# Last column of layer 1 reordered in the twelve seven-product phases, with decodings, W_in's second column, token pieces and stores at other times

## The chip, the cores and the metric

The kernel runs on one core of a Trainium2 chip. The metric is the time of one execution on the device in microseconds (us); it is given as the median of three runs. The engines are TensorE (PE, with its weight loads as PEld), VectorE (DVE), ScalarE (ACT), GpSimd (POOL) and SyncE (SP), which here only issues DMAs.

## The reference

Three stages follow each other, each reading the output of the one before; all of it is float32.

```python
# 1. decayed linear attention, q k v of shape (2, 8, 768, 64)
for t in range(S):
    state = gamma * state + einsum('bhd,bhe->bhde', k[:, :, t], v[:, :, t])
    y[:, :, t] = scale * einsum('bhd,bhde->bhe', q[:, :, t], state)
# 2. mixture of experts on x (1536 x 512), 8 experts, w1 512 x 1024, w2 1024 x 512
P = exp(x @ w_gate - max)              # then 8 rounds of row and column scaling
out = sum over e of P[:, e] * (maximum(x @ w1[e], 0) @ w2[e])
# 3. dense layer, w_in 512 x 2048, w_out 2048 x 512
h = x @ w_in
out = (maximum(h, 0) + alpha * minimum(h, 0)) @ w_out
```

## The kernel before

**Tiling.** The attention fills the first 46 us or so. Then 20 phases follow (`PHASES`, L35), one for each pair of a half of the tokens (768 of 1536) and an expert, or a half of w_in's and w_out's hidden columns. Phases 0 to 7 are half 0 with experts 0 to 7; their first layer is done by the seven products of Strassen and Winograd, their second in the ordinary way. Phases 8 to 15 are half 1 with the experts, and 16 to 19 the dense layer; in these twelve (`FAST`) both layers use seven products. Every float32 product is three matmuls on high and low parts (`mm3`, L300 to L303: high by high is L301, high by low L302, low by high L303).

**A phase.** A phase of the twelve is a row of 56 places on TensorE, each of six matmuls of 128 x 128 by 384 columns. Products of layer 1 are named (column j, product p), with four columns of seven products; column 3 is the last. Units 0 to 27 are layer 2. `fast_order` (L1195 to L1199) and `sequence` (L1201) write the row by hand. Layer 1's sums come out in PSUM; ScalarE copies them out (L947, L967) and VectorE adds to them (L962), or, in the dense layer, makes the slope of the activation (L918 on ScalarE, L919 on VectorE). The blocks b110, b111, b120, b121, b210 and so on are quarters of the hidden layer: `t1` (L1029), `t2` and `t3` (L1033) combine them. Layer 2 then needs fourteen operands hs0 to hs13, each a high half made by ScalarE (`hhigh`, L1055) and a low half made by VectorE (`hlow`, L1063, or L1033 and L1035 for some). Unit u reads hs number u // 2 (hs0 is first read at place 26 or 27, hs1 at 30, hs3 at 34, hs5 at 38, hs12 at 52) with the first and third of its matmuls on the high half and the second (L302) on the low half. So a wait of L302 for hs is one for a low half.

**What sets the order of the other engines.** `step(ph, pos, fn)` (L1209) hangs a piece of work behind the place pos of phase ph; a place of 60 or more belongs to the next phase. Each engine runs what it was given in that order, and a DMA of SP waits in the same way.

**The work hung there, as far as the change touches it.**

- `decode_at` (L1215): W_out and W_in come in a packed form. A piece is loaded (rd, L835), and five VectorE operations (L845, L847, L850, L863, L866) and one of ScalarE (L855) unpack it. Only phases from 1 on have them. Phase 8 has three decodings, at places 5, 17 and 29.
- `w1_at` (L1234): prepares one column n of a later phase's W1 or W_in. Its raw piece (raw0_n) is loaded by `w_load`; four sums (L139) build the combined blocks, then ScalarE makes the high half of the parts a, c and b (L162) and VectorE the low half (L172). The low half of b issues the load of column n + 2 into the buffer that it frees. In phase 15, n + 4 and n + 5 are columns 64 and 65, the first two of W_in for phase 16.
- `x_keep` (L352) and `x_fetch` (L377): pieces of the tokens' combinations. `x_keep` combines them on ScalarE (L366) and GpSimd (L362, L370) and stores them; they are called from phase 16 on, at keys 20, 26, 32 and so on counted in places. `x_fetch` loads them in the phase ahead of their use.
- GpSimd's other work in the twelve phases is the sums of W2's combined blocks (L280, four to a block); the operation L270 of VectorE writes the block dw before them.
- `w1_keep` (L180): stores a prepared piece of W1, so that phases 8 to 15 can load it again (c1). The first ones are collected in `unkept`.

## Time and profile before

| | |
|---|---|
| median of three runs | 1265.24 us |
| lowest and highest | 1264.0 and 1266.26 us |
| the profiled execution's own time | 1265.2 us |
| its span in the trace | 1263.5 us |
| TensorE busy | 1253.4 us, 99% |
| VectorE busy | 999.7 us, 79% |
| ScalarE busy | 652.6 us, 52% |
| GpSimd busy | 454.2 us, 36% |

The profile is one execution taken by the hardware profiler. Its span runs from the first to the last instruction of the trace; 1.7 us of the execution's time lie around it. A group of rows gives the start, the duration, the engine, the line of the code, the operation, and the tiles written and read; in brackets stands the idle time ahead of it on its engine and what ended it.

### The profile page before, as it was taken

To read this page: it belongs to the slowest core of one execution; us is meant where nothing else is said; L and a number is where in the kernel's file an instruction comes from. 1 tells how busy PE (TensorE), PEld (TensorE's weight loads), DVE (VectorE), ACT (ScalarE), POOL (GpSimd) and SP (SyncE) were. 2 spreads that over 40 slices of the span, in tenths; PEclk is the share of its full clock that TensorE was granted. 3 is DMA by queue.
4 is the path that set the end of the run, shared out by engine and by line. 5 is a ranking of instruction groups with operands and counts; after the bars stand their busy time and mean duration, and the time that the engine had idled before them with its cause. 6 is when DMAs were issued, how large, how long until landed. Compare 5 with 4: busy or idle time off the path is not lost.

```text
span 1263.5 us, 20609 instructions
## 1 busy us (share of the span) xinstructions
PE 1253.4 (99%) x7358; PEld 1189.7 (94%) x7358; DVE 999.7 (79%) x1538; ACT 652.6 (52%) x1211; POOL 454.2 (36%) x408
## 2 busy tenths in 40 slices
PE   9999999999999999999999999999999999999998
PEld 7888999989898989899999999999999999999998
DVE  6676888888888888859596967787786989796866
ACT  5644635444444444456455454546464647656573
POOL 5733252526161616101033433252423565551200
PEclk9999999999999999999999999999999999999999
DMA  9784999999999999899999989898989976695615
GB/s 356 260 288 132 329 327 358 326 350 333 341 335 344 336 337 337 278 331 382 329 328 320 337 291 331 290 357 293 355 290 342 332 252 199 231 375 190 215 53 183
DMA packets 230869, 378.15 MB, mean 299 GB/s; under 512 B 16960, under 2 KB 135792, under 8 KB 230768
## 3 DMA queue, kind: packets, MB, share of 16 engines
q1 hardware_dynamic: 230768, 376.85, 87.1%
q8 instruction: 58, 0.95, 0.3%
q14 instruction: 43, 0.35, 0.1%
HBM read 242.54 MB, written 132.67 MB: 297 GB/s over the span
## 4 chain that ended last, share of the span: by engine, by line
PE 93%; DVE 3%; DMA 2%; ACT 1%; issue 0%; SPq 0%; DVEq 0%; ACTq 0%
PE B L302 8%; PE B L301 8%; PE B L303 8%; PE o L301 7%; PE o L303 7%; PE o L302 7%; PE A L301 7%; PE A L302 7%; PE A L303 7%; PE D L302 4%; PE D L301 4%; PE D L303 4%; PE E L301 4%; PE E L303 4%; PE E L302 4%; PE y L581 1%
## 5 line engine op out<-in xcount | busy, mean ns | idle before, releaser
L1055 ACT ACTIVATE hs<-b 128x768 fp32r<-128x768 f32 x168 | 139.5, 842 | 66.5 <-DVE b L1033 18.2
L139 POOL TENSOR_TENSOR raw<-raw 128x256 f32<-128x256 f32 x128 | 125.3, 989 | 100.2 <-DMA raw<-wd 60.7
L1063 DVE TENSOR_TENSOR hs<-b,hs 128x768 fp32r<-128x768 f32 x120 | 119.9, 999 | 9.4 <-ACT hs L1055 9.1
L237 POOL TENSOR_TENSOR pr<-pr 128x256 f32<-128x256 f32 x52 | 52.1, 1002 | 188.7 <-ACT ex L855 62.2
L301 PE MATMUL A<-xh,W 128*128 128x384 f32 x320 | 107.8, 337 | 0.2 <-ACT B L947 0.2
L303 PE MATMUL A<-xh,W 128*128 128x384 f32 x320 | 107.2, 335 | 0.0
L302 PE MATMUL A<-xl,W 128*128 128x384 f32 x320 | 107.0, 335 | 0.0
L162 ACT ACTIVATE W<-raw 128x512 fp32r<-128x512 f32 (+1 forms) x138 | 94.0, 695 | 19.3 <-DVE raw L139 19.3
L302 PE MATMUL B<-hs,ws 128*128 128x384 f32 x288 | 96.8, 336 | 2.0 <-DVE hs L1063 2.0
L370 POOL TENSOR_TENSOR xs<-b,xs 128x384 fp32r<-128x384 f32 x21 | 29.5, 1404 | 191.6 <-ACT xs L366 144.5
L303 PE MATMUL B<-hs,ws 128*128 128x384 f32 x288 | 96.3, 334 | 0.0
L301 PE MATMUL B<-hs,ws 128*128 128x384 f32 x288 | 96.3, 334 | 0.0
L1113 POOL TENSOR_TENSOR total<-total,t 128x384 f32<-128x384 f32 x56 | 71.4, 1303 | 64.5 <-DVE t L1093 64.5
L172 POOL TENSOR_TENSOR W<-raw,W 128x512 fp32r<-128x512 f32 (+1 forms) x49 | 76.1, 1566 | 40.8 <-PE B L303 22.2
L301 PE MATMUL B<-xh,W 128*128 128x384 f32 x268 | 90.6, 338 | 0.0
L280 POOL TENSOR_TENSOR dr<-dr 128x256 f32<-128x256 f32 x32 | 42.3, 1321 | 132.1 <-DMA W<-c 69.1
L303 PE MATMUL B<-xh,W 128*128 128x384 f32 x268 | 89.7, 335 | 0.0
L302 PE MATMUL B<-xl,W 128*128 128x384 f32 x268 | 89.6, 334 | 0.0
L962 DVE TENSOR_TENSOR b<-E,b 128x384 f32<-128x384 f32 x48 | 26.7, 555 | 78.7 <-ACT W L162 48.6
L947 ACT ACTIVATE B<-A 128x384 f32<-128x384 f32 x48 | 22.8, 476 | 121.4 <-PE A L303 121.2
L301 PE MATMUL D<-xh,W 128*128 128x384 f32 x236 | 79.7, 338 | 1.1 <-ACT b L947 1.1
L172 DVE TENSOR_TENSOR W<-raw,W 128x512 fp32r<-128x512 f32 (+1 forms) x89 | 78.2, 895 | 2.8 <-ACT W L162 2.8
(494 smaller groups left out, 3990.2 us busy)
## 6 DMA issues: line engine op xcount, KB each, us to landing
ws<-c SPq DMA_DIRECT2D x168, 512.0 KB, 6.0
raw<-in_w_dram SPq DMA_DIRECT2D x64, 512.0 KB, 5.6
c<-W SPq DMA_DIRECT2D x64, 384.0 KB, 6.4
W<-c SPq DMA_DIRECT2D x88, 256.0 KB, 6.0
pr<-in_w_dram SPq DMA_DIRECT2D x32, 512.0 KB, 5.9
c<-pw SPq DMA_DIRECT2D x32, 512.0 KB, 7.3
c<-pr SPq DMA_DIRECT2D x32, 512.0 KB, 7.9
raws<-in_w_dram SPq DMA_DIRECT2D x32, 384.0 KB, 5.0
```

The lines of the kernel that those rows point to most:

```text
L139: eng.tensor_tensor(out=out, in0=in0, in1=in1, op=op)
L162: nc.scalar.activation(out=hi, in_=src, func=AF.Copy)
L172: eng.tensor_tensor(out=lo, in0=src, in1=hi.bitcast(F32), op=ALU.subtract)
L237: eng.tensor_tensor(out=out, in0=in0, in1=in1, op=op)
L280: nc.gpsimd.tensor_tensor(out=out, in0=in0, in1=in1, op=op)
L301: nc.tensor.matmul(ps, ah, bh, start=first, stop=False, skip_group_check=True)
L302: nc.tensor.matmul(ps, ah, bl, start=False, stop=False, skip_group_check=True)
L303: nc.tensor.matmul(ps, alo, bh, start=False, stop=last, skip_group_check=True)
L370: eng.tensor_tensor(out=t[:, 1], in0=src[q], in1=t[:, 0].bitcast(F32), op=ALU.subtract)
L1055: nc.scalar.activation(out=t[:, 0, :], in_=hsource(ph, k), func=func)
L1063: nc.vector.tensor_tensor(out=lo, in0=src, in1=hi.bitcast(F32), op=ALU.subtract)
L1113: eng.tensor_tensor(out=dst, in0=dst, in1=tt[m, h], op=ALU.add)
```

## The change

The diff does seven things:

1. In the twelve phases the last column's products after (3, 1) and (2, 4) come in the order 6 2 7 5 with (2, 3) behind 5, where they came in the order 2 6 7 and then (2, 3) and 5. Unit 0, product (3, 3) and product (3, 4) come at places 26, 27 and 28; before it was (3, 4), unit 0 and (3, 3).
2. In phases 8 to 15 t1, t2 and t3 of the second pair, and the halves of hs3 and hs5, are hung one place earlier.
3. In phase 8 the second and the third decoding are hung six places later.
4. W_in's second column (n = 65) is prepared in phase 16, with its sums on VectorE, in place of phase 15, where its sums were GpSimd's. The load of column 64 is issued with that of 65, ahead of it. Columns 64 and 67 move too: 64 three places earlier, 67 later.
5. The token pieces of `x_keep` are five, then four places apart in place of six, then five and four.
6. `x_fetch` takes its pieces in another order and at other places.
7. The first stores of W1, kept until then in `unkept`, are issued at the end of the attention.

```diff
@@ -171,6 +171,8 @@
         lo, src, hi = ws1[n].pop(part)
         eng.tensor_tensor(out=lo, in0=src, in1=hi.bitcast(F32), op=ALU.subtract)
         if part == "b" and n != 2 * NJ * E - 2:
+            if n == 2 * NJ * E - 1:
+                w_load(0, n + 1)
             w_load(0, n + 2)
         if n < NJ * E and part != "a":
             unkept.append([2, n, part, hi, lo])
@@ -750,6 +752,8 @@
                     nc.sync.dma_start(out=al, in_=alpha)
                 do_work(g, 3)
             gate_turn(NST // 2 - 2)
+            while unkept:
+                w1_keep(*unkept.pop(0)[1:])
 
 
         ac = ctx.enter_context(tc.tile_pool(name="ac", bufs=1, reuse_waits="tile"))
@@ -1197,10 +1201,11 @@
             fast_order += [(j, 1), (j - 1, 4), (j, 2), (j, 6), (j, 7), (j - 1, 3), (j, 5)]
         fast_order[9], fast_order[10] = fast_order[10], fast_order[9]
         fast_order[16], fast_order[17] = fast_order[17], fast_order[16]
+        fast_order[21:26] = [(NJ - 1, 6), (NJ - 1, 2), (NJ - 1, 7), (NJ - 1, 5), (NJ - 2, 3)]
 
         def sequence(ph):
             if ph in FAST:
-                return fast_order + [(NJ - 1, 4), 0, (NJ - 1, 3)] + list(range(1, 28))
+                return fast_order + [0, (NJ - 1, 3), (NJ - 1, 4)] + list(range(1, 28))
             return order[:27] + slots[:1] + order[27:] + slots[1:]
 
         seq = [sequence(ph) for ph in range(len(PHASES))]
@@ -1256,8 +1261,6 @@
                     prep_at(ph, dve, 31, 31, 31, 33, 34, 34, 35)
                     prep_at(ph, dve, 35, 35, 34, 37, 38, 38, 39)
                     prep_at(ph, pool, 37, 37, 37, 39, 61, 61, 63)
-            if ph == 2 * E - 1:
-                step(ph, 20, lambda: w_load(0, 2 * NJ * E))
             if ph == E - 1:
                 step(ph, 30, lambda: w1_kept(NJ * E))
                 step(ph, 33, lambda: w1_kept(NJ * E + 1))
@@ -1269,9 +1272,12 @@
                 step(ph, 26, lambda m=n + 5: w1_kept(m))
             if fast:
                 w1_at(ph, n + 2, pool, dve, 0, 4, 5, 5, 7, 10, 11)
-                w1_at(ph, n + 3, pool, dve, 5, 10, 12, 12, 14, 17, 18)
-                w1_at(ph, n + 4, pool, dve, 28 if ph == 2 * E - 1 else 18, 36, 38, 39, 40, 42, 43)
-                w1_at(ph, n + 5, pool, dve, 28, 44, 45, 48, 49, 50, 52)
+                w1_at(ph, n + 3, pool, dve, *((12, 13, 14, 17, 18, 18, 20) if ph == 2 * E else (5, 10, 12, 12, 14, 17, 18)))
+                w1_at(ph, n + 4, pool, dve, 25 if ph == 2 * E - 1 else 18, 36, 38, 39, 40, 42, 43)
+                if ph == 2 * E - 1:
+                    w1_at(ph, n + 5, dve, dve, 60, 54, 60, 61, 62, 63, 64)
+                else:
+                    w1_at(ph, n + 5, pool, dve, 28, 44, 45, 48, 49, 50, 52)
             else:
                 if ph:
                     w1_at(ph, n + 2, pool, pool, 0, 3, 3, 6, 6, 9, 9)
@@ -1303,8 +1309,9 @@
             if fast:
                 if ph < E + 2:
                     decode_at(ph, 5, 7, 8, 10)
-                    decode_at(ph, 17, 18, 19, 21)
-                    decode_at(ph, 29, 30, 31, 33)
+                    late_ = 6 * (ph == E)
+                    decode_at(ph, 17 + late_, 18 + late_, 19 + late_, 21 + late_)
+                    decode_at(ph, 29 + late_, 30 + late_, 31 + late_, 33 + late_)
                 else:
                     decode_at(ph, 5, 7, 8, 10)
                     decode_at(ph, 19, 21, 23, 25)
@@ -1317,11 +1324,11 @@
                         step(ph, pos, fn)
                 o = ph < 2 * E
                 for pos, fn, jp in (
-                    (17, t1, 0), (21, t2, 0), (25, t3, 0), (29 - o, t1, 1), (32 - o, t2, 1), (33 - o, t3, 1)
+                    (17, t1, 0), (21, t2, 0), (25, t3, 0), (28 - o, t1, 1), (31 - o, t2, 1), (32 - o, t3, 1)
                 ):
                     step(ph, pos, lambda ph=ph, fn=fn, jp=jp: fn(ph, jp))
-                highs = (11, 23, 19, 30 - o, 22, 33 - o, 32, 34, 36, 38, 41, 43, 47, 49)
-                lows = (13, 26, 20, 31 - o, 24, 34 - o, 33, 35, 37, 39, 42, 44, 48, 50)
+                highs = (11, 23, 19, 29 - o, 22, 32 - o, 32, 34, 36, 38, 41, 43, 47, 49)
+                lows = (13, 26, 20, 30 - o, 24, 33 - o, 33, 35, 37, 39, 42, 44, 48, 50)
                 for k in range(14):
                     step(ph, highs[k], lambda ph=ph, k=k: hhigh(ph, k))
                     step(ph, lows[k], lambda ph=ph, k=k: hlow(ph, k))
@@ -1332,7 +1339,7 @@
                 if ph == 2 * E:
                     for k in range(2):
                         step(ph, 8 + k, lambda k=k: x3.append(x_keep(3, k, *x_copy(k, total))))
-                    for i, key in enumerate((20, 26, 32, 38, 44, 50, 56, 62, 68, 74, 79, 83, 87, 91)):
+                    for i, key in enumerate((20, 25, 30, 35, 40, 45, 50, 55, 60, 65, 70, 74, 78, 82)):
                         for q, pos in enumerate((0, 2, 3, 5)):
                             to = key + pos
                             step(ph + to // 56, to % 56, lambda i=i, q=q: x3[i % 2][i // 2][q]())
@@ -1347,8 +1354,8 @@
             if ph + 1 in XGROUP:
                 g = XGROUP[ph + 1]
                 if g > 1:
-                    for i, pos in enumerate((20, 21, 22, 23, 24, 25, 27, 28, 30, 31, 38, 40, 44, 46)):
-                        q = (B11, B21, T2, T3, T1, B22, T4)[i // 2]
+                    for i, pos in enumerate((20, 21, 22, 23, 24, 25, 26, 27, 28, 30, 34, 36, 43, 45)):
+                        q = (B11, T2, B21, T1, T3, B22, T4)[i // 2]
                         if i % 2 == 0:
                             step(ph, pos, lambda g=g, q=q: new_x(g, q))
                         step(ph, pos, lambda g=g, q=q, w=i % 2: x_fetch(g, q, w))
```

In the orders below a number at the end of a name is left from the tile's own numbering; lines of after are four more than those of before for the same operation, since the change adds four lines above them.

VectorE in phase 12, around the making of the low halves of hs4 and hs1, before and after (b110 and b111 are quarters of the hidden layer, E51 and D51 are PSUM results copied out by ScalarE, dw4 is a block of W2). Before:

```order
925 L866 SCALAR_TENSOR_TENSOR a0_4_1_8680<-rd0_4_1_8584,a0_4_1_8680 128x512
926 L270 TENSOR_TENSOR dw4_8609<-dr4_8541,dw4_8609 128x1024
927 L1063 TENSOR_TENSOR hs12_4_8716<-b110_12_8505,hs12_4_8716 128x768
928 L962 TENSOR_TENSOR b221_12_8653<-E51_8713,b221_12_8653 128x384
929 L1033 SCALAR_TENSOR_TENSOR b120_12_8570<-b220_12_8484,b120_12_8570 128x768
930 L962 TENSOR_TENSOR b211_12_8637<-D51_8718,b211_12_8637 128x384
931 L1063 TENSOR_TENSOR hs12_1_8728<-b111_12_8627,hs12_1_8728 128x768
932 L1029 TENSOR_TENSOR b111_12_8627<-b121_12_8736,b111_12_8627 128x768
```

and after:

```order
925 L870 SCALAR_TENSOR_TENSOR a0_4_1_8680<-rd0_4_1_8584,a0_4_1_8680 128x512
926 L966 TENSOR_TENSOR b221_12_8653<-E51_8704,b221_12_8653 128x384
927 L272 TENSOR_TENSOR dw4_8609<-dr4_8541,dw4_8609 128x1024
928 L1067 TENSOR_TENSOR hs12_4_8716<-b110_12_8505,hs12_4_8716 128x768
929 L1037 SCALAR_TENSOR_TENSOR b120_12_8570<-b220_12_8484,b120_12_8570 128x768
930 L1067 TENSOR_TENSOR hs12_1_8728<-b111_12_8627,hs12_1_8728 128x768
931 L1033 TENSOR_TENSOR b111_12_8627<-b121_12_8747,b111_12_8627 128x768
932 L966 TENSOR_TENSOR b211_12_8637<-D51_8718,b211_12_8637 128x384
```

The add of E51 moved ahead of dw4, and the add of D51 behind hs1 and t1 (the row with L1033 after, L1029 before), so that hs4, t3 and hs1 follow each other.

ScalarE at the seam of phases 15 and 16 (raw0_65 is W_in's second column, B64, D64 and E64 are results of phase 16's first column). Before:

```order
892 L162 ACTIVATE W_144<-raw0_65_10467 128x512
893 L1055 ACTIVATE hs15_12_10806<-b210_15_10297 128x768
894 L162 ACTIVATE W_144<-raw0_65_10467 128x768
895 L1055 ACTIVATE hs15_13_10823<-b211_15_10439 128x768
896 L162 ACTIVATE W_144<-raw0_65_10467 128x512
897 L947 ACTIVATE B64_10887<-A64_10880 128x384
898 L947 ACTIVATE b220_16_10902<-D64_10895 128x384
899 L947 ACTIVATE E64_10912<-B64_10887 128x384
900 L947 ACTIVATE b210_16_10914<-B64_10887 128x384
```

and after:

```order
892 L1059 ACTIVATE hs15_12_10800<-b210_15_10297 128x768
893 L1059 ACTIVATE hs15_13_10815<-b211_15_10439 128x768
894 L162 ACTIVATE W_144<-raw0_65_10469 128x512
895 L951 ACTIVATE B64_10876<-A64_10869 128x384
896 L951 ACTIVATE b220_16_10896<-D64_10889 128x384
897 L162 ACTIVATE W_144<-raw0_65_10469 128x768
898 L951 ACTIVATE E64_10907<-B64_10876 128x384
899 L951 ACTIVATE b210_16_10909<-B64_10876 128x384
900 L922 ACTIVATE n64_00_10920<-A64_10869,sa_76 128x384
901 L162 ACTIVATE W_144<-raw0_65_10469 128x512
```

The three copies of raw0_65 moved from phase 15 into phase 16; the 768-wide one stands between the copy of D64 and the copy of B64 into E64. VectorE's part of it (four sums L139 and then L172) moved to the start of phase 16 in the same way.

VectorE in phase 8, with the second decoding (rd1_7_1, a1_7_1 and ex1_7_1 are its tiles). Before:

```order
663 L863 SCALAR_TENSOR_TENSOR a1_7_1_6230<-a1_7_1_6230,al_74,ex1_7_1_6228 128x512
664 L866 SCALAR_TENSOR_TENSOR a1_7_1_6230<-rd1_7_1_6138,a1_7_1_6230 128x512
665 L962 TENSOR_TENSOR b211_8_6200<-D34_6218,b211_8_6200 128x384
666 L1063 TENSOR_TENSOR hs8_2_6262<-b110_8_6045,hs8_2_6262 128x768
667 L1033 SCALAR_TENSOR_TENSOR b110_8_6045<-b220_8_6017,b110_8_6045 128x768
668 L270 TENSOR_TENSOR dw0_6170<-dr0_6086,dw0_6170 128x1024
669 L1063 TENSOR_TENSOR hs8_4_6303<-b110_8_6045,hs8_4_6303 128x768
670 L962 TENSOR_TENSOR b221_8_6225<-E35_6300,b221_8_6225 128x384
671 L1033 SCALAR_TENSOR_TENSOR b120_8_6124<-b220_8_6017,b120_8_6124 128x768
672 L962 TENSOR_TENSOR b211_8_6200<-D35_6312,b211_8_6200 128x384
673 L1063 TENSOR_TENSOR hs8_1_6320<-b111_8_6190,hs8_1_6320 128x768
```

and after:

```order
663 L849 TENSOR_SCALAR ex1_7_1_6309<-rd1_7_1_6138 128x512
664 L851 TENSOR_SCALAR a1_7_1_6311<-rd1_7_1_6138 128x512
665 L854 SCALAR_TENSOR_TENSOR a1_7_1_6311<-rd1_7_1_6138,a1_7_1_6311 128x512
666 L966 TENSOR_TENSOR b221_8_6225<-E35_6281,b221_8_6225 128x384
667 L272 TENSOR_TENSOR dw0_6170<-dr0_6086,dw0_6170 128x1024
668 L1067 TENSOR_TENSOR hs8_4_6292<-b110_8_6045,hs8_4_6292 128x768
669 L867 SCALAR_TENSOR_TENSOR a1_7_1_6311<-a1_7_1_6311,al_74,ex1_7_1_6309 128x512
670 L870 SCALAR_TENSOR_TENSOR a1_7_1_6311<-rd1_7_1_6138,a1_7_1_6311 128x512
671 L1037 SCALAR_TENSOR_TENSOR b120_8_6124<-b220_8_6017,b120_8_6124 128x768
672 L1067 TENSOR_TENSOR hs8_1_6314<-b111_8_6190,hs8_1_6314 128x768
```

The decoding moved from a place ahead of the low half of hs2 to one on both sides of the low half of hs4, and with the add of E35 ahead of dw0 all but one of the rows between it and hs1 read tiles of SBUF alone.

## Rows read from the trace of the kernel before

**Rows 1.** The page: TensorE's busy time, and its granted clock in 40 slices.

```profile
PE 1253.4 (99%) x7358; PEld 1189.7 (94%) x7358; DVE 999.7 (79%) x1538; ACT 652.6 (52%) x1211; POOL 454.2 (36%) x408
...
PEclk9999999999999999999999999999999999999999
```

**Rows 2.** TensorE's waits over the span: total, times, longest in us.

```profile
PE B L302 <- DVE hs L1063: 2.0, 2, 1.2
...
PE D L301 <- ACT b L947: 1.1, 1, 1.1
...
PE A L302 <- DVE hs L1063: 0.2, 1, 0.2
...
PE A L301 <- ACT B L947: 0.2, 1, 0.2
```

**Rows 3.** Timeline of TensorE: start and duration in us, [idle before <- releaser].

```profile
578.75 0.44 PE L301 MATMUL D<-xh,W 128*128 128x384 f32 x1 [1.10 <-ACT b L947]
...
817.34 0.38 PE L302 MATMUL A<-hs,ws 128*128 128x384 f32 x1
...
1014.19 0.45 PE L302 MATMUL E<-hs,ws 128*128 128x384 f32 x1 [0.46 <-DVE hs L1033]
...
1017.79 0.44 PE L302 MATMUL B<-hs,ws 128*128 128x384 f32 x1 [1.24 <-DVE hs L1063]
...
1058.51 0.45 PE L302 MATMUL D<-hs,ws 128*128 128x384 f32 x1 [0.55 <-DVE hs L1063]
...
1118.40 0.45 PE L302 MATMUL D<-hs,ws 128*128 128x384 f32 x1 [0.20 <-DVE hs L1063]
...
1123.65 0.44 PE L302 MATMUL B<-hs,ws 128*128 128x384 f32 x1 [0.79 <-DVE hs L1063]
```

**Rows 4.** Timeline of VectorE, then of ScalarE, in phase 8.

```profile
570.18 0.43 DVE L845 TENSOR_SCALAR ex<-rd 128x512 uint32<-128x512 uint32 x1 [5.39 <-DMA rd<-in_w_out_dram]
...
577.09 0.85 ACT L1055 ACTIVATE hs<-b 128x768 fp32r<-128x768 f32 x1 [1.96 <-DVE b L1033]
```

**Rows 5.** Timeline of VectorE, then of GpSimd, in phase 12.

```profile
811.70 0.69 DVE L866 SCALAR_TENSOR_TENSOR a<-rd,a 128x512 uint32<-128x512 uint32 x1
812.30 1.22 DVE L270 TENSOR_TENSOR dw<-dr,dw 128x1024 fp32r<-128x1024 f32 x1
813.44 0.95 DVE L1063 TENSOR_TENSOR hs<-b,hs 128x768 fp32r<-128x768 f32 x1
814.31 0.55 DVE L962 TENSOR_TENSOR b<-E,b 128x384 f32<-128x384 f32 x1
814.78 1.02 DVE L1033 SCALAR_TENSOR_TENSOR b<-b,b 128x768 f32<-128x768 f32 x1
...
816.20 1.02 DVE L1063 TENSOR_TENSOR hs<-b,hs 128x768 fp32r<-128x768 f32 x1
817.33 1.31 DVE L1029 TENSOR_TENSOR b<-b,b 128x768 f32<-128x768 f32 x1
...
813.66 5.57 POOL L280 TENSOR_TENSOR dr<-dr 128x256 f32<-128x256 f32 x4 [6.60 <-issue]
```

**Rows 6.** Timeline of VectorE, then of GpSimd, in phase 15.

```profile
998.41 1.49 DVE L1063 TENSOR_TENSOR hs<-b,hs 128x768 fp32r<-128x768 f32 x1
999.82 1.49 DVE L1033 SCALAR_TENSOR_TENSOR hs<-b,hs 128x768 fp32r<-128x768 f32 x1
...
994.12 10.62 POOL L139 TENSOR_TENSOR raw<-raw 128x256 f32<-128x256 f32 x8
```

**Rows 7.** Timeline of TensorE, VectorE, ScalarE, GpSimd at phase 16's start.

```profile
1022.03 0.33 PE L301 MATMUL A<-xh,W 128*128 128x384 f32 x1
...
1027.52 0.56 DVE L962 TENSOR_TENSOR b<-E,b 128x384 f32<-128x384 f32 x1 [3.29 <-PE E L303]
...
1025.37 0.47 ACT L947 ACTIVATE E<-B 128x384 f32<-128x384 f32 x1 [0.55 <-PE B L303]
...
1022.18 4.05 POOL L139 TENSOR_TENSOR raw<-raw 128x256 f32<-128x256 f32 x4
```

## The prediction

> **What bounds the kernel now.** I read the page's busy times first: TensorE is busy 1253.4 us, 99% of the span, at the full granted clock of 2.4 GHz in all 40 slices [rows 1]. The change leaves the count of matmuls alone, so it can only move the few places where TensorE stands still. The list of TensorE's waits is therefore the second view: what the change can reach there is a handful of waits, nearly all for VectorE's low halves of hs (L1063, L1033) and for two copies on ScalarE [rows 2]. The third view is the timeline around each of them [rows 3]. One matmul of 384 columns starts .17 us after the one before and its record lasts .33, so a printed idle time is .16 short of what is lost, and the matmul behind the wait takes .44 instead of .33, another .11. A wait costs its printed idle time and .27. That makes, in phase 8, 1.37 for product 4 of the last column and .47 for the wait of A for ScalarE [rows 2, 3]; at the end of phase 15, .73 and 1.51; in phase 16, .93 (the matmul before it was stretched too, so .38 is added to .55); in phase 17, .47 and 1.06 at hs3 and hs5 [rows 3] and .47 at hs1 (L302 of A, .2 idle) [rows 2]. In phase 12 the same matmul at hs1 has no idle time and lasts .38 [rows 3], about .05 too much; phases 9 to 14 show five or so such places. All of these together are some 7 us, .55% of the time: no gain can be larger.
>
> **Phase 8, the decodings.** VectorE stood 5.39 us for the piece rd that the second decoding reads [rows 4]; hs4 came late, ScalarE's copy of hs4 waited 1.96 for it, and the copy that product 4 needs stood behind that on ScalarE [rows 4]. The decoding moves six places later, 6.3 us, past the landing. The 1.37 goes and, since the same delay made ScalarE's wait at A, most of the .47: 1.7 removed. What is late next: the decoding's five VectorE operations now stand among t2, E's add, dw, hs4, t3 and hs1 (third pair of rows of the order). E's add cannot run before product 5 is done and ScalarE has copied it. In the trace product 5 ends where the idle time ahead of product 4 begins, 577.65 [rows 3]; one place of 1.04 sooner, with the .4 removed ahead of it, is 576.2, and the add's step of .47 ends at about 576.8. From there come dw (a step of 1.14), hs4 (.87), L863 (.60) and L866 (.60), t3 (.87) and hs1 (.95), with the steps of [rows 5], where L863 has L866's shape: 576.8 + 5.03 = 581.8. TensorE reads hs1 four places of 1.04 behind the old place of product 4, which was 577.5 without its wait, so at 581.4 once the .4 ahead is gone: .5 lost without any contention (with rounding), and 2.6 if four of the operations in a row pay .54 to GpSimd (next part). I take 2.2, the GpSimd sums being directly behind dw. Net +.5, from -1.2 to +.9.
>
> **Phases 9 to 14, the last column.** Here two engines meet. Where VectorE runs operations with both inputs in SBUF against GpSimd's sums they alternate: from 998.41 to 999.82 one VectorE operation takes 1.41 [rows 6], where it takes .87 alone (813.44 to 814.31) [rows 5]. A charge is .54. One behind a free slot paid .36 (1.31 instead of .95, at 817.33) and the ones with an add out of PSUM between them only .07 (1.02 instead of .95) [rows 5]. Before, the adds of E and D stood between hs4, t3 and hs1, and GpSimd's four sums (L280) passed under them; hs1 ended at 817.22, and the matmul that reads it began at 817.34, just served [rows 3, 5]. After the change, E's add stands ahead of dw and D's add behind t1 (first pair of rows of the order). Count from 812.30, where L866 lets dw start: E's add .47, dw 1.14, hs4 .87, t3 .87, hs1 .95 gives 816.60, .6 early, with no charge; two charges of .36 give 817.3, .15 late, and two of .54 give 817.7, .5 late. With the refill of .11 a phase costs 0 to .6 more. I take .24, the middle of the two charged cases less the .05 lost before, for the five phases 10 to 14, and nothing for phase 9, whose sums come at another place: +1.2, from -.4 (the small waits all gone) to +2.2. t1 is not urgent, and t2 and t3 move with their products.
>
> The Trainium skill, in "SBUF — State Buffer", section "Who interferes with whom", says that a VectorE instruction with two SBUF inputs contends with a GpSimd instruction that reads SBUF, that the port pair is held for the whole instruction, and that issue order decides who blocks. By that rule three such operations in a row always pay, and the change is worse by the full price in every one of these phases: the slower rival below, which is worked out from the rows alone. Taken at .5 in each, phases 10 to 14 would cost 2.2 in place of 1.2, and the sum would be +1.7 in place of +.7. The trace agrees that they contend, at 1.41 against .87, and shows how little is left of it, 1.02, once an add out of PSUM has given GpSimd its turn.
>
> **End of phase 15.** W_in's second column is no longer prepared here: GpSimd's sums of that column (4 of the 8 at 994.12) [rows 6] and VectorE's subtractions for it leave the stretch, and hs's low halves are back at .87. The .73 and 1.51 at the end go [rows 3]. What remains of GpSimd's work now meets hs1 of this phase instead, one charge less the slack: +.4. Net -1.8, from -2.1 to -1.4. SP now issues the load of W_in's first column ahead of the second's; neither is waited for here.
>
> **Phase 16.** The removed preparation lands here, on an engine with little to do: VectorE had a gap of 3.29 before E's add at 1027.52 [rows 7]. But ScalarE's order puts the 768-wide copy of raw0_65 ahead of the copy of E64 (second pair of rows of the order), and that copy waits for three of VectorE's four sums, which start about .75 after the phase and run against GpSimd's L139 and L1113 (four of L139, 4.05 us from 1022.18) [rows 7]. Four free sums would end in time; at a charge of .54 each the copy starts about 1 us late, and the copy of E64 stood at 3.34 us after the phase's first matmul (1025.37, first matmul at 1022.03) [rows 7], with product 5 behind it at position 4. I take .5, from 0 to 1.2. Beside it: the load of raw0_67 some places later on SP, behind the low half that frees its buffer, so that its low half is just in time (0 to .5, I take .25); hs1 against GpSimd (0 to .5, .25); the token pieces (x_keep) five places apart instead of six, which puts 7 or 8 GpSimd operations where 5 or 6 stood ahead of hs12 (0 to 1.5: up to three charges of .54; I take one). Gone is the .93 at hs3, as the adds L919 moved into VectorE's wait for ScalarE. Sum: .5 + .25 + .25 + .5 - .9 = +.6, from -.9 to +2.5.
>
> **Phases 17, 18 and 0.** In phase 17 five GpSimd operations instead of two or three meet hs1: two or three charges more, +1.3. The .47 and 1.06 at hs3 and hs5 lose most of their cause, as the sums L139 move away from behind them: -1.1. Net +.2, from -1.5 to +1.0. Phase 18 repeats the token pieces at a quiet place: 0, from -.3 to +.2. In phase 0 the four stores of W1 now stand ahead of two loads on SP, and ScalarE's first copy of raw1 moves by as much; TensorE waits for no copy of that kind in the list [rows 2]: 0 to +.2.
>
> **The sum.** .5 + 1.2 - 1.8 + .6 + .2 = +.7 on the profiled execution's 1265.2, which is the median too (1265.24): **1265.9 us**, no change within the 0.2% (2.5 us) that a measurement can tell.
>
> **Rivals.** Faster: no charge falls behind dw, as GpSimd's sums find their slots in VectorE's wait for E and under L270, and hs1 is .6 early as counted above. Then phase 8 gives -1.2, phases 9 to 14 -.4, the end of 15 -2.1, phase 16 -.4 and 17 -.8: -4.9, **1260.3**. For it speaks that before the change hs4, t3 and hs1 paid .07 at the most [rows 5]; against it, that GpSimd starts only when dw has been written, so just ahead of the three. It decides there: GpSimd's first sum must start after hs4 has been issued and be alone with it. Slower: each operation behind dw pays the full .54. It decides from hs1's low half ending later than position 30, where TensorE has no other work in its queue. Phase 8 is +.9, phases 9 to 14 +2.2, the end of 15 -1.6, phase 16 +2.0 (E64's copy and hs12 both late), 17 +.7: +4.2, **1269.4**. For it speaks the steady alternation at 1.41 [rows 6]; against it, the single charge of .36 at 817.33 [rows 5]. That the change does not do what it says is out: the order of the instructions shows each move.
>
> **Chances.** No change .46, faster .24, slower .30: the costs are uncertain by a charge or two per phase, more of them upward. Within the three, the range from 1260.5 to 1270.0 leaves out the lower half of the faster case and the upper quarter of the slower; the likeliest case's own range is 1262.7 to 1267.8.
>
> **What will show it.** In phase 8, no long wait of VectorE for rd; in its place a wait of L302 of A for hs (L1063 before, four lines lower after) of about 2 us. In phases 10 to 14 the same wait at .2 to .3 each; if hs4, t3 and hs1 stand at .95 there, the faster rival holds. At the end of phase 15, no wait over .2. In phase 16, a wait of a matmul for the E64 copy of about .5, and none at hs3. In phase 17 one large wait at hs1 in place of three. The prediction is wrong above all if hs1 of phases 8 and 10 to 14 is in time, or if a DMA, which I have put at nothing outside phase 16, is waited for.

## The result: slower by 0.9%

The changed kernel takes 1277.49 us (median of six runs, 1275.97 to 1279.36) where the kernel before, on the same chip, takes 1266.26. The ratio is 1.0091, 95% interval 1.0078 to 1.0104. The forecast was 1265.9 with a range up to 1270.0, so the time lies outside it, on the side of the slower rival and well beyond that rival's 1269.4.

The profiled execution of the changed kernel took 1279.36 us, 2 above the median, with a span of 1277.3. TensorE has no more to do than before and its clock is the same; the time is in waits. The page's first part and TensorE's list of waits (total, times, longest in us), after the change:

```profile
PE 1254.6 (98%) x7358; PEld 1188.1 (93%) x7358; DVE 1015.1 (79%) x1542; ACT 652.2 (51%) x1211; POOL 450.2 (35%) x404
...
PEclk9999999999999999999999999999999999999999
...
PE A L304 <- DVE hs L1067: 10.0, 10, 2.4
...
PE E L303 <- DVE b L966: 1.4, 2, 1.2
PE E L304 <- DVE hs L1039: 1.0, 1, 1.0
PE B L303 <- DVE E L987: 0.9, 1, 0.9
PE E L303 <- ACT E L951: 0.9, 2, 0.5
```

L304 is the old L302, L1067 the old L1063, L966 the old L962. One line holds most of it: A's low matmul, which reads hs1 at place 30 of a phase, waited .2 once before [rows 2] and waits 10.0 now, in ten phases. New is a wait of E's first matmul (product 3 of the last column) for E's add, L966, and one of E's for ScalarE's copy.

The length of a phase, from its first matmul to the next one's, read from the trace of each kernel, shows where the 13.8 us between the two spans lie. The medians lie 11.2 apart: the profiled execution after is 1.9 above its median, the one before 1.1 below. The last five columns are the difference to before, in us, for kernels that the next section tells of; each is read from one execution.

| phase | before | after, difference | order alone | order undone | sums left out | W_in alone | tokens alone |
|---|---|---|---|---|---|---|---|
| 8 | 62.90 | +0.81 | +2.11 | -0.06 | -1.15 | -0.42 | +0.35 |
| 9 | 58.64 | +2.87 | +1.85 | +0.13 | +0.87 | +0.09 | -0.01 |
| 10 | 58.50 | +0.51 | +1.03 | +0.01 | +0.58 | +0.03 | 0.00 |
| 11 | 58.49 | +1.12 | +0.53 | +0.15 | +0.45 | +1.47 | +0.09 |
| 12 | 58.52 | +1.43 | +1.49 | +0.22 | +0.53 | -0.02 | +0.29 |
| 13 | 58.53 | +0.57 | +0.74 | +0.45 | +1.15 | 0.00 | +0.67 |
| 14 | 58.47 | +1.64 | +0.50 | +0.06 | -0.13 | +0.02 | +0.02 |
| 15 | 60.76 | -0.79 | +0.85 | -1.38 | -1.45 | -1.39 | 0.00 |
| 16 | 59.50 | +4.23 | -0.06 | +4.15 | +4.28 | +2.25 | +2.10 |
| 17 | 60.79 | +0.89 | -0.73 | +1.56 | +0.84 | -0.01 | +1.56 |
| 18 | 58.81 | -0.47 | -0.47 | +0.02 | -0.44 | +0.11 | -0.43 |

The attention and phase 0 together are .8 longer after the change, phase 4 is .5 longer, the other phases are equal to .03. (Phase 8 also holds transposes.) Not every difference is the kernel's. Product 5 of column 2 sometimes waits for a copy that ScalarE makes late, behind a load that landed late: .20, .51 and .71 of phases 11, 12 and 14 after the change, and .85 of the 1.47 of W_in alone in phase 11, a phase which that kernel leaves as it was. It comes and goes from run to run.

**Phase 12**, the place of [rows 5], after the change: VectorE, GpSimd, and the matmul that reads hs1.

```profile
819.22 0.69 DVE L870 SCALAR_TENSOR_TENSOR a<-rd,a 128x512 uint32<-128x512 uint32 x1
819.88 0.56 DVE L966 TENSOR_TENSOR b<-E,b 128x384 f32<-128x384 f32 x1
820.35 1.22 DVE L272 TENSOR_TENSOR dw<-dr,dw 128x1024 fp32r<-128x1024 f32 x1
821.48 0.95 DVE L1067 TENSOR_TENSOR hs<-b,hs 128x768 fp32r<-128x768 f32 x1
822.36 1.50 DVE L1037 SCALAR_TENSOR_TENSOR b<-b,b 128x768 f32<-128x768 f32 x1
823.78 1.49 DVE L1067 TENSOR_TENSOR hs<-b,hs 128x768 fp32r<-128x768 f32 x1
...
821.70 5.57 POOL L282 TENSOR_TENSOR dr<-dr 128x256 f32<-128x256 f32 x4 [7.12 <-issue]
...
825.32 0.45 PE L304 MATMUL A<-hs,ws 128*128 128x384 f32 x1 [0.69 <-DVE hs L1067]
```

VectorE does not idle for an instant. hs4 (the first L1067), issued .22 ahead of GpSimd's first sum, is free (.95), then t3 (L1037) and hs1 (the second L1067) take 1.50 and 1.49 where they took 1.02 each [rows 5]; GpSimd's four sums take 5.57 both times.

**Phase 16**, VectorE, ScalarE and TensorE around product 3 of the last column, after the change:

```profile
1055.12 1.22 DVE L172 TENSOR_TENSOR W<-raw,W 128x512 fp32r<-128x512 f32 x1
1056.27 1.49 DVE L1067 TENSOR_TENSOR hs<-b,hs 128x768 fp32r<-128x768 f32 x1
1057.79 0.96 DVE L1039 TENSOR_TENSOR b<-b,b 128x768 f32<-128x768 f32 x1
...
1060.45 0.56 DVE L966 TENSOR_TENSOR b<-E,b 128x384 f32<-128x384 f32 x1 [0.64 <-ACT b L951]
...
1058.78 0.85 ACT L1059 ACTIVATE hs<-b 128x768 fp32r<-128x768 f32 x1 [2.25 <-DVE b L1039]
1059.54 0.51 ACT L368 ACTIVATE xs<-b 128x384 fp32r<-128x384 f32 x1
1059.95 0.47 ACT L951 ACTIVATE b<-D 128x384 f32<-128x384 f32 x1
...
1061.06 0.44 PE L303 MATMUL E<-xh,W 128*128 128x384 f32 x1 [1.19 <-DVE b L966]
...
1065.87 0.44 PE L304 MATMUL A<-hs,ws 128*128 128x384 f32 x1 [1.22 <-DVE hs L1067]
...
1086.40 0.44 PE L304 MATMUL E<-hs,ws 128*128 128x384 f32 x1 [1.02 <-DVE hs L1039]
```

Column 67's last subtraction (L172) and a charged hs2 (1.49) push t2 (L1039) back; ScalarE's copy for hs4 waits 2.25 for t2, the copy of D stands behind it, E's add waits for that copy, and product 3 for the add. hs1 and, at place 48, hs10 follow late. None of the waits of phase 16 is where the prediction put one of .5: the copy of E64 was in time.

### The profile page after: what moved, and what is told of

It is laid out like the page before. It is cut to its first block, busy times and chain, and to the rows that moved or that the text cites. A ratio compares the mean times of both kernels' runs of the same rounds, so it can differ in the third digit from the quotient of the medians.

```text
span 1277.3 us, 20605 instructions
## 1 busy us (share of the span) xinstructions
PE 1254.6 (98%) x7358; PEld 1188.1 (93%) x7358; DVE 1015.1 (79%) x1542; ACT 652.2 (51%) x1211; POOL 450.2 (35%) x404
## 4 chain that ended last, share of the span: by engine, by line
PE 74%; DVE 11%; DMA 9%; issue 2%; POOL 1%; ACT 1%; SPq 1%; DVEq 0%; POOLq 0%
PE o L303 7%; PE o L305 7%; PE o L304 7%; PE B L303 6%; PE B L304 6%; PE B L305 6%; PE A L304 5%; PE A L305 5%; PE A L303 5%; DVE hs L1067 3%; PE D L304 3%; PE D L305 3%; PE D L303 3%; PE E L303 3%; PE E L305 3%; PE E L304 3%
## 5 line engine op out<-in xcount | busy, mean ns | idle before, releaser
L139 POOL TENSOR_TENSOR raw<-raw 128x256 f32<-128x256 f32 x124 | 121.6, 991 | 132.2 <-DMA raw<-wd 74.7
L1067 DVE TENSOR_TENSOR hs<-b,hs 128x768 fp32r<-128x768 f32 x120 | 125.7, 1048 | 4.7 <-ACT hs L1059 4.3
L304 PE MATMUL A<-xl,W 128*128 128x384 f32 x320 | 107.0, 335 | 0.0
L304 PE MATMUL B<-hs,ws 128*128 128x384 f32 x288 | 96.6, 336 | 0.5 <-DVE hs L1067 0.4
L172 POOL TENSOR_TENSOR W<-raw,W 128x512 fp32r<-128x512 f32 (+1 forms) x49 | 76.3, 1572 | 40.1 <-PE B L305 16.8
L304 PE MATMUL B<-xl,W 128*128 128x384 f32 x268 | 89.6, 334 | 0.0
L966 DVE TENSOR_TENSOR b<-E,b 128x384 f32<-128x384 f32 x48 | 26.7, 555 | 78.3 <-ACT W L162 55.5
L172 DVE TENSOR_TENSOR W<-raw,W 128x512 fp32r<-128x512 f32 (+1 forms) x89 | 79.9, 915 | 2.8 <-ACT W L162 2.8
```

The source lines that it names most:

```text
L139: eng.tensor_tensor(out=out, in0=in0, in1=in1, op=op)
L172: eng.tensor_tensor(out=lo, in0=src, in1=hi.bitcast(F32), op=ALU.subtract)
L304: nc.tensor.matmul(ps, ah, bl, start=False, stop=False, skip_group_check=True)
L1067: nc.vector.tensor_tensor(out=lo, in0=src, in1=hi.bitcast(F32), op=ALU.subtract)
```

## The experiments

Every ratio is to the kernel before on the same chip.

**1. The reordered column alone**, on the kernel before:

```diff
+        fast_order[21:26] = [(NJ - 1, 6), (NJ - 1, 2), (NJ - 1, 7), (NJ - 1, 5), (NJ - 2, 3)]
...
-                return fast_order + [(NJ - 1, 4), 0, (NJ - 1, 3)] + list(range(1, 28))
+                return fast_order + [0, (NJ - 1, 3), (NJ - 1, 4)] + list(range(1, 28))
...
-                    (17, t1, 0), (21, t2, 0), (25, t3, 0), (29 - o, t1, 1), (32 - o, t2, 1), (33 - o, t3, 1)
+                    (17, t1, 0), (21, t2, 0), (25, t3, 0), (28 - o, t1, 1), (31 - o, t2, 1), (32 - o, t3, 1)
```

(and hs3 and hs5 one place earlier, as in the change.)

> The kernel before with the reordered last column and the earlier t1, t2, t3, hs3 and hs5 alone. Theory A (the order causes the loss: the low half of hs1 is late in every one of the twelve phases, and products 3 wait for E's add in phases 9 and 16): about +10 us, with about 2.9 in phase 9, 0.5 to 1.4 in each of phases 10 to 14, and 2 to 3 in phase 16. Theory B (the loss comes from the work that was moved: W_in's second column, token pieces, stores): at most +3 us, and the waits for hs1 in phases 10 to 14 under 0.3 each.

Measured: 1273.21 us, ratio 1.0045 (1.0033 to 1.0057), 6.7 us more. By phases it is +2.11 in phase 8, where the old place of the decodings stays, +1.85 in phase 9, .5 to 1.5 in each of 10 to 14 and .85 in 15, but -.06, -.73 and -.47 in 16 to 18. Theory A holds for phases 8 to 15, though phase 9 came out below its 2.9, and fails for phase 16, so that its +10 was too much: the order alone costs nothing in the dense phases and helps in two of them.

**2. The reordered column undone**, everything else of the change kept: the same diff backwards.

> The changed kernel with the last column, t1, t2, t3, hs3 and hs5 as they were before. Theory A: within 2 us of the kernel before: phase 8 about 1.5 less, the end of phase 15 about 2 less, phase 0 about 1.1 more for the loads behind the stores, phases 16 and 17 up to 2 more. Theory B: +8 us or more.

Measured: 1272.18 us, ratio 1.0044 (1.0031 to 1.0057), 5.7 us more. Neither theory: phases 9 to 14 are as before but for .45 at most, as theory A wants, but phase 8 does not gain the 1.5 (-.06: hs1 waits 1.63 there, with the decodings six places later), phase 16 still loses 4.15 and phase 17 loses 1.56. The order and the moved work each make about half of the loss, in different phases.

**3. GpSimd's sums left out**, on the changed kernel:

```diff
-                nc.gpsimd.tensor_tensor(out=out, in0=in0, in1=in1, op=op)
+                pass
```

> The changed kernel without GpSimd's four sums for W_out's combined blocks in phases 8 to 15 (L282 in it, L280 before), so that those blocks are wrong; everything else is as in the changed kernel. Theory C (contention: t3 and hs1 each pay about 0.54 to those sums): t3 and hs1 go from 1.49 back to 0.95, the wait at hs1 in phases 10 to 14 falls from 0.6 to 0.95 to under 0.3, and the time falls by 5 to 7 us. Theory D (VectorE gets there late whatever GpSimd does, behind E's add and the 1.14 us of dw): the waits stay above 0.5 and the time falls by less than 2 us.

Measured: 1271.67 us, ratio 1.0040 (1.0029 to 1.0051), 5.8 below the changed kernel's median. VectorE in phase 12 of this kernel:

```profile
814.43 0.56 DVE L966 TENSOR_TENSOR b<-E,b 128x384 f32<-128x384 f32 x1
814.90 1.22 DVE L272 TENSOR_TENSOR dw<-dr,dw 128x1024 fp32r<-128x1024 f32 x1
816.04 0.95 DVE L1067 TENSOR_TENSOR hs<-b,hs 128x768 fp32r<-128x768 f32 x1
816.90 0.95 DVE L1037 SCALAR_TENSOR_TENSOR b<-b,b 128x768 f32<-128x768 f32 x1
817.78 0.95 DVE L1067 TENSOR_TENSOR hs<-b,hs 128x768 fp32r<-128x768 f32 x1
```

From the add's start to hs1's end it is 4.30 here and 5.39 after the change (819.88 to 825.27): two charges of .54. The time lost at hs1 in phases 8 to 15, 9.0 us after the change (start to start of the matmuls, less .17), is 1.6 here. Theory C is shown, D is not: VectorE's own chain is only .2 to .3 late in four phases and .6 in phase 8.

**4. dw and the sums later**, on the changed kernel (the third and fourth number are the places of dw and of the sums):

```diff
-                    for pos, fn in zip((6, 12, 24, 27, 40, 52), dense_prep(ph - E)):
+                    for pos, fn in zip((6, 12, 31, 32, 40, 52), dense_prep(ph - E)):
```

> The changed kernel with the subtraction dw (L272 in it) and the sums behind it hung seven places later, behind hs3, and its stores with it. Both the 1.14 us of dw and the sums are then gone from the path to hs1. Theory C: the wait at hs1 vanishes in phases 8 to 15 (9 us less), and 1 to 3 us come back at hs5 and behind, where the sums now run. Theory D gives the same for dw itself, 1.14 a phase, so 5 to 7 us less. If the sums collide as badly later on, the time stays within 2 us.

Measured: 1278.79 us, ratio 1.0096 (1.0070 to 1.0122): no better than the change. The wait at hs1 is gone from phases 8 to 15, as expected of C, but the time returns elsewhere, more of it than expected: 1.67 in phase 8 and 1.89 in phase 9 at unit 16, 1.03 at hs5 in phase 9, .4 to .7 at hs12 in phases 9, 10, 12, 13 and 15. The list of waits of this kernel, and VectorE and TensorE at unit 16 of phase 9:

```profile
PE B L304 <- DVE hs L1067: 2.9, 6, 0.9
PE A L304 <- DVE hs L1067: 2.3, 2, 1.2
PE B L303 <- ACT xs L368: 1.7, 1, 1.7
...
PE B L303 <- ACT W L162: 1.5, 1, 1.5
...
659.14 1.76 DVE L1067 TENSOR_TENSOR hs<-b,hs 128x768 fp32r<-128x768 f32 x1
660.83 0.55 DVE L1147 TENSOR_TENSOR E<-B,d 128x384 f32<-128x384 f32 x1
...
661.48 0.41 PE L303 MATMUL B<-hs,ws 128*128 128x384 f32 x1 [1.73 <-ACT xs L368]
```

The list names ScalarE at unit 16. But unit 16 writes B, and VectorE's read of B (L1147) ends .1 ahead of the matmul, at 661.38 here and at 598.49 for 598.60 in phase 8; it stands behind charged operations, so this is the likelier cause. In phases 10 to 15 together this trace loses .5 where the one after the change loses 4.5; phase 9 alone loses 4.95 in place of 2.87. The two traces are not equal partners, 2.1 below the median here and 1.9 above it there, so the medians decide on the whole; whether dw could stay late with phase 9 spared was not tried.

**5. E's add between hs4 and t3 again**, on the changed kernel, with TensorE's new order:

```diff
-                    for pos, fn in zip((6, 12, 24, 27, 40, 52), dense_prep(ph - E)):
+                    for pos, fn in zip((6, 12, 23, 27, 40, 52), dense_prep(ph - E)):
...
-                lows = (13, 26, 20, 30 - o, 24, 33 - o, 33, 35, 37, 39, 42, 44, 48, 50)
+                lows = (13, 26, 20, 30 - o, 24 - o, 33 - o, 33, 35, 37, 39, 42, 44, 48, 50)
```

> The changed kernel with the subtraction dw and the low half of hs4 one place earlier in phases 8 to 15, so that E's add, which reads PSUM, stands between hs4 and t3 again; TensorE's order is the changed one. Theory C with its slot (an operation out of PSUM gives GpSimd a turn that costs VectorE nothing): one of the two charges of 0.54 goes, the wait at hs1 falls by 0.4 to 0.6 in phases 8 and 10 to 15, 3 to 4 us less in all. Rival (the order of VectorE does not matter, GpSimd's four sums are paid once in any order): within 1 us of the changed kernel.

Measured: 1278.24 us, ratio 1.0092 (1.0076 to 1.0108), the same as the change; by the total the rival, by the rows theory C. VectorE, GpSimd and TensorE in its phase 12:

```profile
817.04 1.22 DVE L272 TENSOR_TENSOR dw<-dr,dw 128x1024 fp32r<-128x1024 f32 x1
818.17 0.95 DVE L1067 TENSOR_TENSOR hs<-b,hs 128x768 fp32r<-128x768 f32 x1
819.04 0.55 DVE L966 TENSOR_TENSOR b<-E,b 128x384 f32<-128x384 f32 x1
819.51 1.02 DVE L1037 SCALAR_TENSOR_TENSOR b<-b,b 128x768 f32<-128x768 f32 x1
820.45 1.49 DVE L1067 TENSOR_TENSOR hs<-b,hs 128x768 fp32r<-128x768 f32 x1
...
818.39 5.55 POOL L282 TENSOR_TENSOR dr<-dr 128x256 f32<-128x256 f32 x4 [6.61 <-issue]
...
819.65 0.44 PE L303 MATMUL E<-xh,W 128*128 128x384 f32 x1 [1.11 <-DVE b L966]
```

t3 is back at 1.02, and the wait at hs1 is gone in phases 9 to 15. In its place product 3 waits 1.0 to 1.9 in each of them, since it accumulates into E and E's add, now behind dw and hs4, must have read E first. From dw and E's add to hs1's end it is 4.90 in place of 5.39, one charge less; the rest of hs1's wait went because TensorE, held up at product 3, reads hs1 later. In the list the wait of product 3 has grown to 8.4 us:

```profile
PE E L303 <- DVE b L966: 8.4, 8, 1.8
PE A L304 <- DVE hs L1067: 3.1, 3, 1.2
```

So in neither of these two orders is the new row of TensorE had for nothing. Product 3 one place sooner moves the time by which E's add must be done 1.04 us ahead. Put the add first and hs1 is late; put dw and hs4 first and product 3 is late. The rows leave VectorE no idle time from dw to hs1.

**6. hs4's high half one place later**, on the changed kernel (23 in place of 22 in `highs`):

> The changed kernel with the high half of hs4 hung one place later, so that ScalarE copies D into b22 ahead of it and no longer makes that copy wait for t2 of VectorE. Theory G (E's add, and with it product 3 and hs1, hangs on this chain in phases 9 and 16): the wait of product 3 for E's add, 0.33 and 1.36, goes, hs1 of these two phases comes 0.5 to 1.3 sooner, 2 to 4 us less in all, and the other phases stay. Theory C (two charges of 0.54 in a row make hs1 late): under 1.5 us less, as the charges stay; hs4's low half may come later and cost some of it.

Measured: 1279.02 us, ratio 1.0103 (1.0081 to 1.0125), not below the change. In phase 9 the wait for E's add is gone and hs1's loss falls from 1.40 to .27, as theory G has it; in phase 16 product 3 still loses 1.35 and hs1 2.36 in place of 1.39. There E's add no longer waits for ScalarE, but VectorE itself is as late, behind column 67 and charged operations (t2 takes 1.67 in place of .96), so taking the chain through ScalarE away gains nothing. And the low half of hs4 now waits 1.18 for the later high half, in phases 16 and 17: hs1 of phase 17 loses 2.55 in place of 1.30. Behind that wait the granted clock fell to .50, the lower level of 1.2 GHz, from 1126.6 to 1130.0, which cost some 1.6 us more in this execution. G holds for phase 9 alone.

**7. W_in's second column alone**, on the kernel before:

```diff
-            if ph == 2 * E - 1:
-                step(ph, 20, lambda: w_load(0, 2 * NJ * E))
...
+                if ph == 2 * E - 1:
+                    w1_at(ph, n + 5, dve, dve, 60, 54, 60, 61, 62, 63, 64)
```

(with the new places of columns 64 and 67 and the load of 64 ahead of 65, as in the change.)

> The kernel before with W_in's second column prepared in phase 16 and the loads of columns 64 and 67 moved with it, nothing else. Theory E (this move does the damage of phase 16): the end of phase 15 gains 1.4 to 2.2, phase 16 loses 2 to 4, with a wait of product 4 of the last column for the copy behind hs4, about 1.8; in all +1 to +2.5 us. Theory F (the damage of phase 16 is the closer token pieces): -1.5 us.

Measured: 1267.11 us, ratio 1.0004 (.9994 to 1.0013), between the totals of the two theories. Phase 15 gains 1.39, the least that E expected, and phase 16 loses 2.25. The loss is theory E's: product 4 of the last column in phase 16 waits for the copy of D behind hs4, with the chain of after over again:

```profile
1049.34 0.84 ACT L1057 ACTIVATE hs<-b 128x768 fp32r<-128x768 f32 x1 [2.17 <-DVE b L1037]
1050.09 0.51 ACT L368 ACTIVATE xs<-b 128x384 fp32r<-128x384 f32 x1
1050.50 0.47 ACT L949 ACTIVATE b<-D 128x384 f32<-128x384 f32 x1
...
1051.02 0.44 PE L303 MATMUL D<-xh,W 128*128 128x384 f32 x1 [1.66 <-ACT b L949]
```

(In this kernel lines are two further than before.) Columns 65 and 67 move together here; which of them makes the loss was not told apart.

**8. The token pieces alone**, on the kernel before:

```diff
-                    for i, key in enumerate((20, 26, 32, 38, 44, 50, 56, 62, 68, 74, 79, 83, 87, 91)):
+                    for i, key in enumerate((20, 25, 30, 35, 40, 45, 50, 55, 60, 65, 70, 74, 78, 82)):
```

(with `x_fetch` in its new order.)

> The kernel before with the token pieces of x_keep closer together and x_fetch in the other order, nothing else. Theory E: phases 16 and 17 lose 1 to 2.5 us, at hs10 to hs12 of phase 16 and at hs1, hs3 and hs5 of phase 17. Theory F: +4 to +6 us, most of it in phase 16 at place 26 and places 48 to 52.

Measured: 1269.39 us, ratio 1.0024 (1.0013 to 1.0036), 2.5 us more. Phase 16 loses 2.10, at places 48 and 50 (.42 and .93) and in small ones; phase 17 loses 1.56, .4 to .7 more at each of hs1, hs3 and hs5. The places are theory E's; the size is at its upper end by the median and above it in the two phases of the trace (3.66). VectorE ahead of place 50 of phase 16, and the matmul there:

```profile
1071.15 1.77 DVE L172 TENSOR_TENSOR W<-raw,W 128x768 fp32r<-128x768 f32 x1
1072.85 1.77 DVE L1035 TENSOR_TENSOR hs<-b,hs 128x768 fp32r<-128x768 f32 x1
1074.54 1.51 DVE L172 TENSOR_TENSOR W<-raw,W 128x512 fp32r<-128x512 f32 x1
1075.97 1.76 DVE L1035 TENSOR_TENSOR hs<-b,hs 128x768 fp32r<-128x768 f32 x1
...
1077.79 0.44 PE L302 MATMUL E<-hs,ws 128*128 128x384 f32 x1 [0.76 <-DVE hs L1035]
```

Beside the token pieces, sums of 128 x 384 on GpSimd, the 128 x 768 operation takes 1.77 in place of .95: a charge is .82 here, not .54, and four stand in a row where before there were two (1.51 at 1071.76 and 1.76 at 1073.19). With experiment 7, phase 16's 4.2 is about the sum of two moves, 2.25 and 2.10, and the order has no part in it.

**9. The decodings twelve places later**, on the kernel before, with the earlier column order:

```diff
-                    decode_at(ph, 17, 18, 19, 21)
-                    decode_at(ph, 29, 30, 31, 33)
+                    late_ = 12 * (ph == E)
+                    decode_at(ph, 17 + late_, 18 + late_, 19 + late_, 21 + late_)
+                    decode_at(ph, 29 + late_, 30 + late_, 31 + late_, 33 + late_)
```

> The kernel before with the second and third decoding of phase 8 twelve places later in place of six, so behind hs1. Theory C: at six places the decoding pushes VectorE's operations into GpSimd's sums and gives the 1.7 us back at hs1; behind hs1 it does not, and phase 8 gains 1.3 to 1.7 us. Rival: the decoding then makes hs3 or hs5 late, which are read 3.5 and 7.5 places on, and the gain is under 0.5.

Measured: 1266.97 us, ratio 1.0004 (.9994 to 1.0014). Phase 8 gains 1.32, as theory C expects, where six places gained .06 (experiment 2); the profiled run gives .82 back in phase 9, at product 4, where rd lands late again. The same wait of phase 9, 1.14, stands in the trace of experiment 10, where no decoding was moved, so it comes and goes. The gain does not show in the median.

**10. The stores alone**, on the kernel before:

```diff
             gate_turn(NST // 2 - 2)
+            while unkept:
+                w1_keep(*unkept.pop(0)[1:])
```

> The kernel before with the first four stores of W1 issued ahead of the two loads of raw1, nothing else. Theory: 0.5 to 1.1 us more at the first copy of raw1 in phase 0 (product at place 14), and a wait of 0.3 to 0.5 in phase 4; +1 us in all. Rival: phase 0 only differs by how the attention ends, and the time stays within 0.3 us.

Measured: 1266.81 us, ratio 1.0004 (.9991 to 1.0016): no difference that can be told. The attention and phase 0 are .87 longer in its trace, .8 in that of after. Of the seven traces with the stores six are .6 to 1.0 longer there and one (experiment 2) is not, and no trace without them is more than .2 longer, so this may be real. Phase 4's .5 came up as well in kernels without the stores (experiments 11 and 12), so it is not theirs. The profiled execution, 1271.93, is the slowest of ten: in phase 14 product 5 of column 2 waited 2.02 behind the late load, and from 928.2 to 931.7 the granted clock was .52, the lower level of 1.2 GHz; that phase is 3.8 longer, though this kernel leaves it as it was.

**11. The new order in the dense phases alone**, on the kernel before: the row of experiment 1 for phases 16 to 19 and the old one for 8 to 15.

> The kernel before with the reordered last column and the earlier t1, t2, t3, hs3 and hs5 in the dense phases 16 to 19 alone, where no sums of W_out's blocks run. Theory C (the order costs time only where those sums run): phases 8 to 15 as before, phase 16 within 0.3, phase 17 0.7 less, phase 18 0.5 less, about -1.2 us. Rival (the order is late by itself): +0.5 to +2 us in phases 16 to 18.

Measured: 1265.56 us, ratio .9995 (.9985 to 1.0005). The phases are what theory C expects, -.02, -.76 and -.47 in 16 to 18, and all others as before but for .4 to .6 at single places; 1.2 us is too little for the interval to show.

**12. The same, and only the subtractions of W_in's second column moved:**

```diff
-                w1_at(ph, n + 5, pool, dve, 28, 44, 45, 48, 49, 50, 52)
+                w1_at(ph, n + 5, pool, dve, 28, *((44, 60, 48, 60, 50, 61) if ph == 2 * E - 1 else (44, 45, 48, 49, 50, 52)))
-                w1_at(ph, n + 3, pool, dve, 5, 10, 12, 12, 14, 17, 18)
+                w1_at(ph, n + 3, pool, dve, *((9, 12, 13, 14, 16, 17, 18) if ph == 2 * E else (5, 10, 12, 12, 14, 17, 18)))
```

> As the one before, and of W_in's second column only the three subtractions (L172) moved to the start of phase 16, its sums staying GpSimd's in phase 15; column 67's sums 4 places later. Theory: VectorE is early enough at the end of phase 15, so the waits of 0.73 and 1.51 there fall by 1.5 to 2.2, and the subtractions fill VectorE's idle 3.29 in phase 16 for nothing; -2.5 to -3.5 us against the kernel before. Rival: column 67 becomes late as in the changed kernel, phase 16 loses 1 to 2 at product 4 and product 3, and the sum is near -1.

Measured: 1265.13 us against 1266.69, ratio .9986 (.9975 to .9997), 1.6 us less: the lowest median of all, below the kernel before by little more than the interval and not to be told from experiment 11, and short of the 2.5 to 3.5 expected. Phase 15 gains .74 only: .61 and .78 are still lost at hs11 and hs12, and hs11 takes 1.76 at 1012.62, beside GpSimd's L1113; the column's own sums had ended at 1004.99. Phase 16 loses .30 with 1.24 at hs1, and phases 17 and 18 keep their .73 and .47.

## Why the prediction was wrong

**What held.** The mechanism of the slower rival, GpSimd's sums charged to operations of VectorE that follow each other, is the one at work: .54 an operation, at t3 and hs1, in every phase from 8 to 15 (experiment 3). Of the operations behind dw only these two pay; hs4, already issued when GpSimd starts, does not. The place of the wait, L302 of A for hs1, was named for all of them, and phase 8 came out at +.8 for +.5: without the sums hs1 is .57 late there, for .5 in the working. Phase 18's sign was missed by little, -.5 for 0.

**Phases 9 to 14: mis-sized, +8.1 for +1.2.** Two steps failed, beside a slip in the sum: .24 a phase leaves out the refill of .11 that stands a sentence ahead of it. The term took the middle of .15 and .5 late, less what was lost before; the rows show the upper end and more, .54 to .85 in phases 10 to 14 and .11 of refill. The charge of .36, which I had from t1, came up again at t1 alone (1.30), behind hs1; at t3 and hs1 all charges were .54. And the count began at the end of L866 as if it always ended 5.04 us ahead of hs1's matmul, as in the trace of before. After the change E's add starts 4.90 and 4.85 ahead of it in phases 10 and 13, and 4.6 in 11, 12 and 14 (819.88 to 824.46 in phase 12). With 4.30 for the chain and two charges that is the .54 and .60 of phases 10 and 13, and the whole of their loss. In the other three VectorE's row from t1 to hs1 starts later still. The row below shows it: t1 waits for a copy of ScalarE's, which stood behind the load that landed late, and from there to hs1 no idle time takes that up.

```profile
812.41 0.96 DVE L1033 TENSOR_TENSOR b<-b,b 128x768 f32<-128x768 f32 x1 [3.84 <-ACT b L971]
```

That load is a DMA waited for, one of the prediction's own signs of being wrong; as it comes and goes between runs, it is not shown to be the change's.

The second step is phase 9, taken at nothing because its sums "come at another place". They stand at the same place and cost 1.5 at hs1 with the refill, and E's add, behind a copy that ScalarE makes behind hs4, made product 3 wait too (.33); unit 16 and hs12 lost .34 and .59. I had not asked of E's add who waits for it, other than hs1: TensorE does, at product 3, and in experiment 5 that costs 1.0 to 1.9 a phase.

**The end of phase 15: -.8 for -1.8.** The two waits went, as forecast; hs1 lost 1.48 where I had taken .4. It is the same error as in phases 9 to 14.

**Phase 16: +4.2 for +.6, the largest miss.** The wait for the copy of E64, at .5, did not come at all. Column 67's late place I had at .25; with W_in's second column it costs 2.25 (experiment 7). The rows there show a chain of four steps from VectorE to ScalarE and on to a matmul, which I had not followed beyond the first; in the changed kernel VectorE is as late without ScalarE's part (experiment 6), so how much each step adds there is open. The token pieces, one charge of .54 by my count, cost 2.1 here (experiment 8): two more charges of .82 ahead of place 50. The trace of before has this price, 1.76 at 1073.19, and I had taken that of the 128 x 256 sums. The gain at hs3 came: no loss over .15 is left there.

**Phase 17: +.9 for +.2.** hs1 lost 1.4 with the refill and hs5's wait went, as forecast, but hs3 lost more than before, .82 for .47, and a wait for a copy at place 14 grew from .2 to .8.

**The range.** The terms' upper ends add up to +5.6, 1270.8, so the range to 1270.0 kept most of them. The ends themselves were too low: phase 9 had no term and lost 2.87, phases 10 to 14 lost 5.3 for 2.2 at most, phase 16 lost 4.2 for 2.5, and the end of phase 15 gained .8 for 1.4 at least. Most of this hangs on one thing, charges on a VectorE that has no idle time, and so the terms went the same way together.

The parts measured alone make 6.7 (order), .3 (W_in), 2.5 (tokens) and .1 (stores), and by phase 8 about -1.3 for the decodings: 8.3 us of the 11.2. The intervals of the parts are 1.2 to 1.6 to either side each, so the rest is neither shown nor excluded as an interaction.

## What to carry to other kernels

Where an engine of the second rank runs without idle time between two operands that TensorE waits for, moving a product one place sooner is not free: ask which reads of its accumulator must be done first, and add the whole place to what that engine has to fit in. Where two engines contend, count every operation behind the start of the other one's work at the full price, read that price for the very pair of operations (.54 and .82 here), and look for the operation between them that lets the other one have its turn. And when work is moved into a quiet stretch, follow its last instruction through each queue up to a matmul; in experiment 7 the damage came four steps later and not at the first one.

## What the runs showed of the hardware that was not expected

The same operation, t3 of 128 x 768 against the same sums of GpSimd, takes 1.02 us behind an add that reads PSUM (experiment 5) and 1.50 behind one that reads only SBUF (after), while GpSimd's four sums take 5.55 and 5.57: the order on VectorE decides whether VectorE pays, and GpSimd takes no longer for it. The Trainium skill, "SBUF — State Buffer", section "Who interferes with whom", says that issue order and not the shape of the operation decides who blocks; these two rows agree.

A charge goes by the other engine's operation: the same 128 x 768 operation takes .95 alone, 1.49 beside GpSimd's 128 x 256 sums and 1.77 beside its 128 x 384 sums (experiment 8).

Twice the granted clock fell to the lower level, .50 and .52 for some 3.5 us, soon after TensorE had stood 2.38 and 2.02 us (experiments 6 and 10), with matmuls .32 apart in place of .17. After the change TensorE stood 2.37 us in phase 8 and the clock stayed at 1.00, so a stand of that length does not always bring it.
